# Queries and keys turned by two DMA transposes a batch, scores from 64x64 blocks in fours, a third value buffer

## The chip, the core and the metric

The kernel runs on one core of a Trainium2 chip. The metric is device time in microseconds (us); lower is better. Tensor work is done by TensorE (PE in the profile; its weight loads are listed as PEld), element-wise work by VectorE (DVE), ScalarE (ACT) and GpSimd (POOL). SyncE (SP) issues DMAs only; POOL issues DMAs as well, between its element-wise instructions. Every engine runs its own instructions strictly in the order in which the program lists them.

## The reference, cut to what matters

Sliding-window causal attention (window 64) over 8 batches, 8 heads, 576 rows, head size 64, and behind it a two-layer feed-forward block whose activation is h*cos(h), over all 8*576 = 4608 rows.

```
scores = scale * matmul(q, k.transpose(0, 1, 3, 2))
mask = (rel >= 0) & (rel < 64)            # rel = query row - key row
scores = where(mask, scores, -1e9); scores -= max(scores)
attn = exp(scores); attn = attn / (sum(attn) + 1e-9)
x = matmul(attn, v)                       # to 4608 x 512
h = x @ w_in;  g = h * cos(h);  out = g @ w_out     # 512 -> 2048 -> 512
```

Inputs and output are float32; on the chip the matmul operands are bf16.

## The kernel before, in words

**Tiles.** The feed-forward block works on nine tiles (`mt` 0 to 8) of 512 rows. A stage of the program is one `mt`: first 64 matmuls 128x128 by 512 columns that make `h_ps` (`first`, L338 to L342), each of 16 banks followed by a sine on ACT (L486) and a product on DVE (L489) that makes `gT`; then 64 matmuls of the same size that make `out_ps` (L501). I call them the h phase and the out phase. Attention of batch t+1 is woven into stage t, for t from 0 to 6: its scores, softmax and transposes run beside stage t, and its weighted values (`values`, L314) and their copies `xT` (`put_x`, L325) come at the end of the stage, as the next stage's `first` reads `xT`. Stages 7 and 8 hold no scores.

**A unit** is one batch, a pair of heads and one block of 64 query rows against 128 key rows; a batch has 9 blocks and 4 pairs, so 36 units. `groups` (L221 to L229, sizes from `CUTS`) puts 3 or 4 units together. For each group there are `g_scores` (PE, L232), `g_max` (DVE: mask and row maximum, a custom instruction for each unit, L268), `g_exp` (ACT, L279), `g_inv` (DVE), `g_norm` (POOL, L293) and `g_trans` (a DMA transpose on SP that makes `wT`, L305; for a few groups of batches 0 and 1 by PE, L302).

**How q and k get their head size onto the partitions.** Batches 0 and 1: PE transposes of 64x64 (L177). Batches 2 to 7: `load_chunk` (L142) loads q and k as 6 chunks of 96 rows each, in bf16. q is then turned by PE, 6 transposes for each pair of heads (L180), into PSUM, and two DVE copies for each pair (`put_block`, L199) write it into `qblocks`, where the two heads of a pair stand on the diagonal of a 128x128 block whose other half was set to zero (`clear`, L348, and L432). So one matmul 128x128 by 128 columns gives the scores of both heads (L248). k is turned by 6 DMA transposes on SP (`turn_k`, L212) for batches 3 to 7, by PE and ACT copies for batch 2. Batch 0 and 1 scores are made from two 64x64 matmuls a unit (L254).

**v** lies in two buffers; the rows between the loaded 128-row chunks are copied inside SBUF by `spread_v` (L156), on POOL for batches 3 to 7.

**Order.** It is written by hand. Stage 0 begins with the list `FIRST`; for the rest, `at(time, fn, ...)` (L368) puts a step into a plan, and `pump(time)` (L371), called after each sine-and-product step of the h phase and after each fourth matmul of the out phase, emits all steps that are due. A stage has `T` = 32 units of planned time, 16 for each phase, and begins at `T * mt`. So a step planned at `t0 + 14.6` stands right behind the h phase on its engine's queue. All loads are issued by POOL (in order with `g_norm`), the DMA transposes and the stores of finished rows by SP (in order with one another). PSUM has five named banks and three turning ones (`ps_t`, tag "t").

The score matmuls before, for batches 2 and up:

```
nc.tensor.matmul(out=s_ps[:, u].rearrange("p (a t) -> p a t", a=2),
                 lhsT=qblocks[(b % 2) * PAIRS + p][:, j].rearrange("d h t -> d (h t)"), rhs=rhs,
                 start=True, stop=True, skip_group_check=True)
```

Of the kernel before, what the change touches and what calls it, by code (L numbers as in the profile page):

```python
# [10 lines left out]
def _safe_warn(msg, *a, **kw):  # L11
# [12 lines left out]
NU = 9  # L24
NC, NP = 6, 96
# [3 lines left out]
CUTS = (  # L29
# [7 lines left out]
)  # L37
# [21 lines left out]
def kernel(  # L59
# [45 lines left out]
    H_BANKS = ("O1", "X0", "X1", "S", "O0") * 3 + ("X0",)  # L105
    S_BANKS = ("X1", "S", "X0")
    S_FIRST = ("O1", "S", "O0", "X0", "X1")

    def bank(which, name):
        return ps.tile([128, 512], F32, tag=which, name=name)  # L110
# [21 lines left out]
    def rows_tile(name):  # L132
        return ld.tile([128, NC * H * D], BF16, tag=name, name=name)

    def load_heads(name, b, p0=0, n=PAIRS):
        if (name, b) not in st:
            st[name, b] = rows_tile(name)[:, 0:PAIRS * RC * D].rearrange("p (a x) -> p a x", a=PAIRS)
        src = {"q": q, "k": k}[name][b, 2 * p0:2 * p0 + 2 * n]
        nc.gpsimd.dma_start(out=st[name, b][:, p0:p0 + n],
                            in_=src.rearrange("(a h) (p c) d -> (h p) a (c d)", h=2, c=RC))  # L140

    def load_chunk(name, b, c):  # L142
        if (name, b) not in st:
            st[name, b] = rows_tile(name)[0:NP].rearrange("p (c x) -> p c x", c=NC)
        src = {"q": q, "k": k}[name][b, :, c * NP:c * NP + NP]
        nc.gpsimd.dma_start(out=st[name, b][:, c].rearrange("p (h d) -> p h d", h=H),  # L146
                            in_=src.rearrange("h p d -> p h d"))

    def load_v(b, c):
        n = 128 if c < 4 else 64  # L150
        vt = vtiles[b % 2][:n, 2 * c if c < 4 else 2 * c - 1]
        nc.gpsimd.dma_start(out=vt.rearrange("p (h d) -> p h d", h=H),  # L152
                            in_=v[b, :, c * 128:c * 128 + n, :].rearrange("h p d -> p h d"))


    def spread_v(b, half, engine="p"):  # L156
        vt = vtiles[b % 2]
# [12 lines left out]
    def transposed(name, b, p):  # L170
        t_ps = ps_t.tile([128, S], BF16, tag="t", name=f"t{name}_ps")
        of = st[name, b]
        if b < 2:
            for c in range(RC):
                for h in range(2):
                    d = slice(64 * h, 64 * h + 64)
                    nc.tensor.transpose(t_ps[d, 64 * c:64 * c + 64], of[d, p, 64 * c:64 * c + 64], ident[d, d])  # L177
        else:
            for c in range(NC):
                nc.tensor.transpose(t_ps[:, NP * c:NP * c + NP], of[:, c, 128 * p:128 * p + 128], ident[:NP, :NP])  # L180
        return t_ps


    def in_order(t_ps, to, b):
        return (t_ps.rearrange("d (c p) -> d p c", c=RC), to.rearrange("d (p c) -> d p c", c=RC)) if b < 2 else (t_ps, to)

    def tr_q(b, p):
        st["tq", b, p] = transposed("q", b, p)

    def put_q(b, p, engine=None):  # L190
        of, to = in_order(st.pop(("tq", b, p)), qtiles[b * PAIRS + p], b)
        if b:
# [6 lines left out]
    def put_block(b, p, h):  # L199
        d = slice(64 * h, 64 * h + 64)  # L200
        copy("d", qblocks[(b % 2) * PAIRS + p][d, :, h], st["tq", b, p][d].rearrange("d (j t) -> d j t", j=NU))

    def tr_k(b, p):
        st["tk", b, p] = transposed("k", b, p)

    def k_tile(b):
        if ("kA", b) not in st:
            st["kA", b] = ka = att.tile([128, PAIRS, S], BF16, tag="kT", name="kT", bufs=2)
            st.update({("kT", b, p): ka[:, p] for p in range(PAIRS)})
        return st["kA", b]  # L210

    def turn_k(b, c):  # L212
        nc.sync.dma_start(out=k_tile(b)[:, :, c * NP:c * NP + NP], in_=st["k", b][:, c], transpose=True)

    def put_k(b, p, engine="a"):
        kt = k_tile(b)[:, p]
        of, to = in_order(st.pop(("tk", b, p)), kt, b)
        copy(engine, to, of)
# [13 lines left out]
    def g_scores(n, which):  # L232
        s_ps = bank(S_FIRST[which] if n < n_first else S_BANKS[which], "s_ps")
        units = groups[n]
        s_ps = s_ps[:, 0:len(units) * 128].rearrange("p (u c) -> p u c", c=128)
        if n < n_first:
            m0 = 2 if units[0][2] else 0
            nc.tensor.matmul(out=s_ps.rearrange("p u c -> p (u c)"), lhsT=ident,
                             rhs=mask16[:, m0:m0 + len(units)].rearrange("p u c -> p (u c)"),
                             start=True, stop=False, skip_group_check=True)  # L240
        for u, (b, p, j) in enumerate(units):
            kt = st["kT", b, p]
            lo = max(64 * j - 64, 0)
            rhs = kt[:, lo:lo + 128].rearrange("d (a t) -> d a t", a=2)
            if j and j % 2 == 0:
                rhs = rhs[:, ::-1, :]
            if b > 1:
                nc.tensor.matmul(out=s_ps[:, u].rearrange("p (a t) -> p a t", a=2),  # L248
                                 lhsT=qblocks[(b % 2) * PAIRS + p][:, j].rearrange("d h t -> d (h t)"), rhs=rhs,
                                 start=True, stop=True, skip_group_check=True)  # L250
                continue
            for h in range(2):
                d = slice(64 * h, 64 * h + 64)
                nc.tensor.matmul(out=s_ps[d, u].rearrange("p (a t) -> p a t", a=2),  # L254
                                 lhsT=qtiles[b * PAIRS + p][d, 64 * j:64 * j + 64], rhs=rhs[d], start=n >= n_first,
                                 stop=n >= n_first or u == len(units) - 1, skip_group_check=True)
        st["s", n] = s_ps

# [55 lines left out]
    def values(mt, p):  # L314
        st["o", mt, p] = o_ps = bank("S", "o_ps") if mt > 1 and p == PAIRS - 1 else ps_t.tile([128, MT], F32, tag="t", name="o_ps")
        for i in range(TU):
            b, j = divmod(mt * TU + i, NU)
            wT = st["wT", (b, p, j)]
            for h in range(2):
                nc.tensor.matmul(out=o_ps[64 * h:64 * h + 64, 64 * i:64 * i + 64],  # L320
                                 lhsT=vtiles[b % 2][:, max(j - 1, 0), 128 * p + 64 * h:128 * p + 64 * h + 64],
                                 rhs=wT[:, 64 * h:64 * h + 64], start=True, stop=True, skip_group_check=True)
# [15 lines left out]
    def first(mt, ff, ks, start, stop):  # L338
        if start:
            st["h", ff] = bank(H_BANKS[ff], "h_ps")  # L340
# [7 lines left out]
    def clear(i):  # L348
        nc.gpsimd.memset(qblocks[i].rearrange("d j h t -> d (j h t)"), 0.0)

    def last_rows(gT, o_sb):
        ms = MT // 128 - 1
        for which, lo, hi in (("O0", 0, LAST), ("S", LAST, d_model)):
# [26 lines left out]
    for t in range(B - 1):  # L380
        last = max(i for i, units in enumerate(groups) if units[0][0] == t + 1)
        time = T * t + Q - 1.4
        for i in range(last + 1 - n):
            time += PACE * len(groups[n - 1]) if i else 0
            at(time - 1.05 * (i % 2) * (t == 0), g_scores, n, i % 3)
# [9 lines left out]
    for b in range(1, B):  # L395
        t0 = T * (b - 1)
        for p in range(PAIRS):
            t_q = 7 + 1.8 * p if b == 1 else t0 + 1 + 2.5 * p if b == 2 else t0 + 1 + 3.5 * p
            steps = (((0, tr_q), (0.01, tr_k), (0.02, put_q), (0.03, put_k)) if b == 1 else
                     ((0, tr_q), (0.02, put_block, 0), (0.5, put_block, 1)) +  # L400
                     (((9.5 - 0.8 * p, tr_k), (9.51 - 0.8 * p, put_k)) if b == 2 else ()))
            for lag, fn, *args in steps:
                at(t_q + lag, fn, b, p, *args)
        if b > 1:
            for c in range(NC):
                for i, name in enumerate(("q", "k")):
                    at(t0 - T + (5.6 + 1.6 * c + 0.8 * i if b > 2 else 27.5 + 0.9 * c if i else 4 + 0.5 * c), load_chunk, name, b, c)
            for c in range(NC if b > 2 else 0):
                at(t0 - 5.5 + c, turn_k, b, c)
            for c in range(5):  # L410
                at(t0 + 0.5 + c, load_v, b, c)
            for half in range(2):
                at(t0 + (14.45 + 0.1 * half if b > 2 else 10), spread_v, b, half, "p" if b > 2 else "dma")
    for half in range(2):
        at(17.5, spread_v, 1, half, "dma")
    for p in range(PAIRS):
        at(T + 3 + 4 * p, clear, PAIRS + p)
# [13 lines left out]
    for t in qblocks[:PAIRS]:  # L431
# [109 lines left out]
```

## Time and profile before

| What | Value |
|---|---|
| Time, median of 3 runs (all) | 318.29 us (317.81, 318.29, 319.23) |
| Span of the profiled execution, first to last instruction | 316.6 us |
| What lies around the span, taken as median less span | 1.7 us |
| PE busy | 300.1 us, 95% of the span |
| ACT, DVE, POOL busy | 238.3, 227.8, 196.6 us |
| Start of `first` of stages 0 to 8, in us of the span | 26.43, 61.99, 95.59, 129.25, 160.59, 192.62, 224.62, 256.61, 285.63 |

The profile is of one execution of its own, for which only the span is known; the median is of other executions. The rows of a view read: line, engine, operation, tiles and shapes, count, then busy time and the mean of one instruction; "idle before" names the time that the engine stood still just ahead and what ended it. The chain of waits is the work that ended last, followed back from the last instruction; its rows are start, duration, what. Matmuls are pipelined, so the mean duration of one (379 ns for 512 columns) is longer than the distance from one to the next.

### The profile page before, as it was taken

The numbers are of one execution on the slowest core, as the hardware profiler recorded it, in microseconds if no ns is written. First come the engines' busy times: TensorE is split into PE (matmuls) and PEld (weight loads), VectorE is DVE, ScalarE is ACT, GpSimd is POOL, SyncE is SP. The second block draws the span as 40 slices with busy tenths as digits, with TensorE's granted clock in tenths as the row PEclk, the third lists the DMA queues.
The fourth block names the chain that finished last, engine by engine and source line by source line (L and its number), as shares of the span: only waits on it lengthen the run. The fifth ranks groups of instructions, "written<-read, shape, count | busy, mean of one in ns | idle before, by whom it ended". The sixth has DMA issues, their size and how long they took to land.

```text
span 316.6 us, 7858 instructions
## 1 busy us (share of the span) xinstructions
PE 300.1 (95%) x2580; PEld 157.5 (50%) x2620; DVE 227.8 (72%) x871; ACT 238.3 (75%) x789; POOL 196.6 (62%) x228
## 2 busy tenths in 40 slices
PE   3678999999999999999999999999999999999995
PEld 2544545555555544545554555555555554454443
DVE  5976778689767977697859885997599758335801
ACT  3978689868998689869986998699868996115600
POOL 8896156799969767897788878986832630000000
PEclk9979999999999999999999999999999999999999
DMA  6999996699959994899989997999692442011011
GB/s 97 170 211 207 207 148 90 70 194 162 160 92 98 151 228 85 88 153 231 124 91 140 230 123 83 158 218 127 77 179 92 81 105 100 2 66 69 0 66 66
DMA packets 150697, 39.91 MB, mean 126 GB/s; under 512 B 139392, under 2 KB 146176, under 8 KB 150656
## 3 DMA queue, kind: packets, MB, share of 16 engines
q0 software_dynamic: 99824, 18.36, 75.7%
q1 hardware_dynamic: 50688, 20.85, 32.5%
q8 instruction: 20, 0.33, 0.4%
q14 instruction: 21, 0.17, 0.2%
q10 hardware_dynamic: 144, 0.20, 0.2%
HBM read 36.70 MB, written 9.44 MB: 146 GB/s over the span
## 4 chain that ended last, share of the span: by engine, by line
PE 81%; DVE 6%; ACT 5%; POOL 3%; issue 2%; DMA 2%; POOLq 0%
PE h_ps L341 35%; PE out_ps L501 34%; ACT e L279 3%; PE s_ps L248 3%; DVE gT L489 3%; PE o_ps L320 3%; DMA k<-in_k_dram 2%; PE tq_ps L180 2%; PE s_ps L254 1%; POOL w L293 1%; PE out_ps L356 1%; DVE qB L113 1%; PE tw_ps L302 1%; POOL v L113 1%; PE tk_ps L177 1%
## 5 line engine op out<-in xcount | busy, mean ns | idle before, releaser
L341 PE MATMUL h_ps<-xT,w_in 128*128 128x512 bf16 x556 | 130.5, 379 | 2.9 <-ACT xT L113 1.0
L501 PE MATMUL out_ps<-w_out,gT 128*128 128x512 bf16 x543 | 130.9, 379 | 1.2 <-issue 0.5
L486 ACT ACTIVATE sin<-h_ps 128x512 f32<-128x512 f32 x144 | 83.6, 598 | 39.2 <-PE h_ps L341 36.2
L489 DVE TENSOR_TENSOR gT<-h_ps,sin 128x512 bf16<-128x512 f32 x144 | 92.2, 685 | 27.1 <-ACT sin L486 26.2
L279 ACT ACTIVATE e<-s,negm 128x128 f32<-128x128 f32 x256 | 98.7, 388 | 1.0 <-DVE negm L268 0.9
L293 POOL TENSOR_TENSOR w<-e,rden 128x512 bf16<-128x512 f32 (+1 forms) x78 | 74.0, 958 | 35.6 <-DVE rden L286 29.1
L341 PEld LDWEIGHTS <-w_in 128*128 128x128 bf16 x576 | 54.3, 98 | 60.7 <-issue 2.4
L501 PEld LDWEIGHTS <-gT 128*128 128x128 bf16 x560 | 51.5, 98 | 49.7
L268 DVE CUSTOM_DVE_ANT_0 s<-s_ps,mask 128x128 f32<-128x128 f32 x256 | 58.2, 285 | 1.9 <-PE s_ps L254 1.6
L279 ACT ACTIVATION_READ_ACCUMULATOR e<-s,negm 128x1 f32 x256 | 48.1, 188 | 0.0
L146 POOL DMA_DIRECT2D q<-in_q_dram x36 | 28.9, 804 | 12.3 <-PE h_ps L341 4.7
L152 POOL DMA_DIRECT2D v<-in_v_dram x40 | 34.1, 874 | 3.0 <-DMA k<-in_k_dram 2.0
L146 POOL DMA_DIRECT2D k<-in_k_dram x36 | 29.0, 806 | 3.2 <-DMA k<-in_k_dram 2.4
L113 ACT COPY out_sb<-out_ps 128x512 f32<-128x512 f32 (+1 forms) x18 | 10.1, 563 | 25.7 <-PE out_ps L501 20.2
L286 DVE RECIPROCAL rden<-den 128x4 f32<-128x4 f32 (+1 forms) x80 | 13.9, 173 | 20.9 <-ACT e L279 18.3
L113 DVE CAST xT<-o_ps 128x512 bf16<-128x512 f32 x27 | 17.5, 678 | 9.9 <-PE o_ps L320 9.9
L113 DVE COPY out_sb<-out_ps 128x512 f32<-128x512 f32 x18 | 12.4, 689 | 16.6 <-PE out_ps L501 12.6
L248 PEld LDWEIGHTS <-qB 128*128 128x128 bf16 x216 | 17.0, 98 | 14.6 <-DVE negm L268 0.6
L113 POOL COPY v<-v 64x2048 bf16<-64x2048 bf16 (+1 forms) x11 | 18.7, 1701 | 5.4 <-DMA v<-in_v_dram 5.0
L248 PE MATMUL s_ps<-kT,qB 128*128 128x128 bf16 x216 | 21.9, 219 | 0.2 <-DVE negm L268 0.2
L113 DVE COPY qB<-tq_ps 64x576 bf16<-64x576 bf16 x48 | 21.6, 450 | 0.3
L268 DVE DVE_READ_ACCUMULATOR2_ANT negm<- 128x1 f32 x256 | 21.3, 83 | 0.0
(57 smaller groups left out, 187.5 us busy)
## 6 DMA issues: line engine op xcount, KB each, us to landing
out_dram<-out_sb SPq DMA_DIRECT2D x16, 512.0 KB, 6.8
v<-in_v_dram POOLq DMA_DIRECT2D x32, 128.0 KB, 6.2
q<-in_q_dram POOLq DMA_DIRECT2D x36, 96.0 KB, 7.1
k<-in_k_dram POOLq DMA_DIRECT2D x36, 96.0 KB, 7.5
w_out<-in_moe_w_out_dram POOLq DMA_DIRECT2D x2, 1024.0 KB, 16.4
w_in<-in_moe_w_in_dram POOLq DMA_DIRECT2D x2, 768.0 KB, 11.8
wT<-w SPq DMA_TRANSPOSE x66, 2.9
out_dram<-out_sb SPq DMA_DIRECT2D x3, 256.0 KB, 2.0
```

The lines of the kernel that those rows point to most:

```text
L113: {"a": nc.scalar.copy, "p": nc.gpsimd.tensor_copy}.get(engine, nc.vector.tensor_copy)(out, in_)
L146: nc.gpsimd.dma_start(out=st[name, b][:, c].rearrange("p (h d) -> p h d", h=H), in_=src.rearrange("h p d -> p h d"))
L152: nc.gpsimd.dma_start(out=vt.rearrange("p (h d) -> p h d", h=H), in_=v[b, :, c * 128:c * 128 + n, :].rearrange("h p d -> p h d"))
L248: nc.tensor.matmul(out=s_ps[:, u].rearrange("p (a t) -> p a t", a=2), lhsT=qblocks[(b % 2) * PAIRS + p][:, j].rearrange("d h t -> d (h t)" ...
L268: nc.vector.tensor_tensor_reduce(out=s[:, u], in0=s_ps[:, u], in1=mask[:, 2 - j % 2 if j else 0], scale=-scale if b else -1.0, scalar=BIG, ...
L279: nc.scalar.activation(e[:, u], s[:, u], AF.Exp, bias=negm[:, u:u + 1], scale=1.0 if n < n_first else -1.0, accum_out=den[:, u:u + 1])
L286: nc.vector.reciprocal(out=rden[:, 0:len(groups[n])], in_=den[:, 0:len(groups[n])])
L293: (nc.gpsimd if engine == "p" else nc.vector).tensor_tensor(out=w[:, 0:u], in0=e[:, 0:u], op=ALU.mult, in1=rden[:, 0:u].unsqueeze(2).to_br ...
L341: nc.tensor.matmul(out=st["h", ff], lhsT=w_in_sb[:, ks, ff * 128:ff * 128 + 128], rhs=st["xT", mt][:, ks], start=start, stop=stop)
L486: nc.scalar.activation(sin, h_ps, AF.Sin, bias=math.pi / 2.0)
L489: nc.vector.tensor_tensor(out=gt[:, e], in0=h_ps, in1=sin, op=ALU.mult)
L501: nc.tensor.matmul(out=o_ps[e], lhsT=gT[ff // 2][:, ff % 2, ms * 128:ms * 128 + 128], rhs=w_out_sb[:, ff], start=ff == 0, stop=ff == n_ff - 1)
```

## The change

q and k of batches 2 to 7 are loaded as 128-row chunks into nine slots of one tile `rows` (slots 0 to 3 q, 5 to 8 k; slot 4 holds the last 64 rows of q on partitions 0 to 63 and those of k on 64 to 127). Two DMA transposes on SP turn the tile, slots 0 to 4 and slots 5 to 8, at planned time `t0 + 1.6` and `t0 + 1.7` of the stage that needs them. `qblocks`, `put_block`, `clear`, `turn_k` and the PE transposes of these batches go. Scores of batches 1 to 7 are made by `burst`: two groups together, each unit from two 64x64 blocks, the second group's blocks with the head halves crossed over on the output side, so that four consecutive matmuls use four different quarters of the PE array. In stages 1 to 6 there are two bursts (4 groups at `t0 + 14.6`, 6 groups 24 `out_ps` matmuls later) in place of ten single groups; in stage 0 the groups go two by two. Batch 1's PE transposes are paired in the same way. v gets a third buffer, and `spread_v` goes from POOL to DVE, at `t0 + 12.3` and `t0 + 13.3`, which puts the two copies ahead of the last two products of the h phase. The banks of `h_ps` and `out_ps` are dealt out anew.

As built, SP's order in stages 2 to 6 is: the previous batch's `wT` transposes, the two stores of 512 KB, the two turns, then this batch's ten `wT` transposes. In stage 1 the two turns stand ahead of the two stores. POOL's order in a stage is: last products of the previous batch, 5 v loads, 5 q loads, 5 k loads (for the batch that the next stage scores; none in stage 6), then the products of this batch.

```
-    qtiles = [const.tile([128, S], BF16, name=f"qT{i}") for i in range(2 * PAIRS)]
-    qblocks = [const.tile([128, NU, 2, 64], BF16, name=f"qB{i}") for i in range(2 * PAIRS)]
-    vtiles = [const.tile([128, NU - 1, d_model], BF16, name=f"v{i}") for i in range(2)]
+    vtiles = [const.tile([128, NU - 1, d_model], BF16, name=f"v{i}") for i in range(3)]
...
+CUTS = (FIRST_CUT,) + ((((1, 0, 4),), ((2, 4, 6),), ((1, 6, 9),)),) * 6
+    H_FIRST = ("O1", "X0", "X1", "S", "O0") * 3 + ("X0",)
+    H_BANKS = ("X0", "O0", "X1", "S", "O1") * 2 + ("X0", "X1", "S", "O0", "O1", "t")
+    BURSTS = (("X0", "X1", "S", "t"), ("X0", "X1", "S", "t", "t", "t"))
...
     def load_chunk(name, b, c):
+        n = 128 if c < 4 else 64
+        lo = 64 if c == 4 and name == "k" else 0
+        slot = c + (5 if c < 4 and name == "k" else 0)
+        nc.gpsimd.dma_start(out=rows(b)[lo:lo + n, slot * 512:slot * 512 + 512].rearrange("p (h d) -> p h d", h=H),
+                            in_={"q": q, "k": k}[name][b, :, c * 128:c * 128 + n].rearrange("h p d -> p h d"))
+
+    def turn(b, lo, hi):
+        nc.sync.dma_start(out=turned(b)[:, lo * 512:hi * 512].rearrange("d (g x) -> d g x", x=128),
+                          in_=rows(b)[:, lo * 512:hi * 512], transpose=True)
...
+    def burst(n0, banks):
+        for i in range(0, len(banks), 2):
+            pair = [groups[n0 + i], groups[n0 + i + 1]]
+            s_ps = [bank(which, "s_ps")[:, 0:len(pair[0]) * 128].rearrange("p (u c) -> p u c", c=128)
+                    for which in banks[i:i + 2]]
+            for u in range(len(pair[0])):
+                for cross in range(2):
+                    b, p, j = pair[cross][u]
+                    for h in range(2):
+                        d, to = slice(64 * h, 64 * h + 64), slice(64 * (h ^ cross), 64 * (h ^ cross) + 64)
+                        nc.tensor.matmul(out=s_ps[cross][to, u].rearrange("p (a t) -> p a t", a=2),
+                                         lhsT=q_cols(b, p, j)[d], rhs=k_cols(b, p, j)[d],
+                                         start=True, stop=True, skip_group_check=True)
...
+        if t:
+            at(times[0], burst, n, BURSTS[0])
+            at(times[4] + 0.1, burst, n + 4, BURSTS[1])
+        else:
+            for i in range(0, last + 1 - n, 2):
+                at(times[max(i - 1, 0)] + (0.5 if i else 0), burst, n + i, (S_BANKS[i % 3], S_BANKS[(i + 1) % 3]))
...
+    for b in range(2, B):
         t0 = T * (b - 1)
+        for c in range(NC):
+            for i, name in enumerate(("q", "k")):
+                at(t0 - T + 4 + (0 if b == 2 else 4.5) + 0.9 * (5 * i + c), load_chunk, name, b, c)
+            at(t0 + 4 + 0.9 * c, load_v, b, c)
+        at(t0 + 1.6, turn, b, 0, 5)
+        at(t0 + 1.7, turn, b, 5, 9)
+        for half in range(2):
+            at(t0 + 12.3 + half, spread_v, b, half, "d")
...
-    for t in qblocks[:PAIRS]:
-        nc.vector.memset(t.rearrange("d j h t -> d (j h t)"), 0.0)
```

More of the change, by code (lines that the diff above doesn't have):

```diff
@@ L232, in g_scores @@
     def g_scores(n, which):
-        s_ps = bank(S_FIRST[which] if n < n_first else S_BANKS[which], "s_ps")
+        s_ps = bank(S_FIRST[which], "s_ps")
         units = groups[n]
         s_ps = s_ps[:, 0:len(units) * 128].rearrange("p (u c) -> p u c", c=128)
[L236 to L240, printed above, removed]
@@ L241, in g_scores @@
-        for u, (b, p, j) in enumerate(units):
[L242 to L251, printed above, removed]
+        m0 = 2 if units[0][2] else 0
@@ L493 @@
             o_sb = moe.tile([128, 2, d_model], F32, tag="out", name="out_sb", bufs=2)
[L494 removed]
+            o_ps = [bank(which, "out_ps") for which in (("O0",) if mt == n_mt - 1 and ms0 else ("O0", "O1"))]
             for step, (lo, e) in enumerate([(lo, e) for lo in range(0, n_ff, half) for e in range(2)]):
```

164 lines of the change are left out of this document (77 added, 87 removed), and 7 rows, old and new, of the table CUTS.

## The prediction, made before the changed kernel was run

> **What bounds it now.** I read the page first, then the busy times cut at the stages, then the chain of waits inside one stage.
>
> ```profile
> PE 300.1 (95%) x2580; PEld 157.5 (50%) x2620; DVE 227.8 (72%) x871; ACT 238.3 (75%) x789; POOL 196.6 (62%) x228
> PEclk9979999999999999999999999999999999999999
> ```
>
> PE is busy 95% of the span at full granted clock, so what is taken off PE can count. The first and the last of the six stages that hold the changed work (row = start:end, length, then busy us of PE, PEld, DVE, ACT, POOL):
>
> ```profile
> 61.99:95.59 33.60, 33.35 (x305) 18.08 (x307) 26.44 (x114) 29.34 (x98) 30.68 (x36) 1.00 1.56 148
> ...
> 224.62:256.61 31.99, 31.75 (x248) 16.64 (x252) 25.75 (x113) 27.36 (x95) 17.06 (x17) 1.00 0.72 109
> ```
>
> Stages 1 to 6 take 256.61 - 61.99 = 194.6 us together, 32.4 each, and PE has work in nearly all of it (33.35 of 33.60, 31.75 of 31.99). The chain through stage 4 stays on PE all the way:
>
> ```profile
> 160.59 1.06 PE h_ps L341 x4
> ...
> 163.38 0.26 PE tq_ps L180 x6
> ...
> 175.64 0.22 PE s_ps L248 x4
> ...
> 181.71 0.17 PE s_ps L248 x3
> ...
> 188.01 3.45 PE out_ps L501 x16
> ...
> 192.62 1.02 PE h_ps L341 x4
> ```
>
> So the h phase lasts 175.64 - 160.59 = 15.05 us and the out phase 192.62 - 175.64 = 16.98. One large matmul costs 3.45 / 16 = 0.216 us. Four blocks of q transposes cost 4 * 0.26 = 1.04 us; ten score groups (six of four units, four of three) cost 6 * 0.22 + 4 * 0.17 = 2.0.
>
> ACT stands close behind PE:
>
> ```profile
> 175.68 0.60 ACT L486 ACTIVATE sin<-h_ps 128x512 f32<-128x512 f32 x1 [0.27 <-PE h_ps L341]
> 177.69 0.39 ACT L279 ACTIVATE e<-s,negm 128x128 f32<-128x128 f32 x1
> 192.03 0.57 ACT L113 COPY out_sb<-out_ps 128x512 f32<-128x512 f32 x1
> 192.49 0.58 ACT L113 CAST xT<-o_ps 128x512 bf16<-128x512 f32 x1
> ```
>
> Its exponentials start 2.05 us after the h phase's end, run without a gap to 192.03, and the `xT` copy ends at 193.07. PE needs that copy for the fourth matmul of the next stage, 3 * 0.216 = 0.65 us after 192.62: a slack of 0.2 us.
>
> **The parts, on PE and ACT.** Let S be a stage's first `h_ps` matmul and H the end of its h phase.
>
> The q transposes go in stages 1 to 6, so H = S + 14.0 in place of 15.05 (in stage 1 k's go too). Scores become 72 matmuls of 64x64 a stage. The two-at-a-time form is in stage 0:
>
> ```profile
> 34.94 0.40 PE tq_ps L177 x18
> ```
> ```profile
> 42.50 0.56 PE s_ps L254 x16
> ...
> 45.76 0.45 PE s_ps L254 x12
> ```
>
> (0.56 - 0.45) / 4 = 0.028 us a matmul, and 0.11 for entering a block. Four at a time I take half of that, as all four quarters work: 72 * 0.014 + 2 * 0.11 = 1.2 us in place of 2.0. The other end is no overlap beyond two, 72 * 0.028 + 0.22 = 2.2. The out phase on PE is then 16.2 us.
>
> In the Trainium skill, TensorEngine Tiling (Array Packing), section "Restrictions and Gotchas", speaks against this: different row tiles cannot access the same PSUM bank at the same time. By it the two row halves would go one after the other. The two-at-a-time blocks above already write one bank from both row halves, and 0.028 is half of what one 128-column matmul of the 128x128 form costs (0.22 / 4 = 0.056): the trace does not bear the rule out for this shape.
>
> ACT's work after H is unchanged. DVE gets the two v copies ahead of the last two products, and loses eight `qB` copies:
>
> ```profile
> 175.21 1.88 DVE L489 TENSOR_TENSOR gT<-h_ps,sin 128x512 bf16<-128x512 f32 x3
> ```
> ```profile
> 0.96 2.36 DVE L432 MEMSET qB<- 128x576 uint32 x4
> ```
> ```profile
> 19.09 1.23 DVE L113 COPY v<-v 64x1536 bf16<-64x1536 bf16 x1
> ```
> ```profile
> 18.75 3.33 POOL L293 TENSOR_TENSOR w<-e,rden 128x512 bf16<-128x512 f32 x3
> ```
>
> The last three products of this h phase run back to back (1.88 us), so a copy put ahead of the last two delays them by its whole length. The one DVE copy of v took 1.23 us, beside a POOL instruction that had 0.7 us left (3.33 / 3 = 1.11 each, from 18.75). If it waited for that, the copy alone is 0.5 us; if not, 1.2 and by size 1.6. I take 0.5 and 0.65, as POOL only issues DMAs at that place: the first exponential moves from H + 2.05 to about H + 2.2, and the next stage can start at H + 17.1 by ACT, H + 16.2 by PE. The high end (2.8 us) would cost 1.7 us a stage where nothing else is late. POOL's relief and the third v buffer I cost at nothing: POOL is not on the stage's chain, and its v loads start right behind the last product (below), with no wait for a v buffer. The fills that zeroed `qblocks` ran on DVE from 0.96 to 3.32, while nothing but loads was on its way; nothing too, with some tenths as the other end. Batch 1's halved blocks and transposes in stage 0 are worth 80 * 0.014 = 1.1 us and something between nothing and 4 * 0.40; I take 1.4 in all (ends 0.5 and 2.5).
>
> With every load in time a stage takes 14.0 + 17.1 = 31.1 us.
>
> **The part that decides: two big DMA transposes.** The turns are due by H, because the first burst needs both, and behind that burst the whole out phase is queued on PE. How far do they get in 14 us?
>
> ```profile
> 172.28 1.23 SPq L364 DMA_DIRECT2D out_dram<-out_sb  x2
> ```
> ```profile
> 194.28 1.20 SPq L305 DMA_TRANSPOSE wT<-w  x1
> ```
> ```profile
> 192.73 1.04 POOL L293 TENSOR_TENSOR w<-e,rden 128x512 bf16<-128x512 f32 x1 [0.95 <-DVE rden L286]
> 193.71 4.27 POOL L152 DMA_DIRECT2D v<-in_v_dram  x5
> ```
>
> The last product of a stage ends at S + 1.15, its `wT` transpose occupies SP for 1.2, the two stores for 1.23: the first turn is issued at S + 3.6. Stores and turns share SP's queue (q1). POOL issues its loads (q0) from S + 1.1 on. How the two queues share the 16 DMA engines is seen in narrow windows of the DMA view; packets and MB, first beside transposes (0.5 us), then beside the stores (2 us), then transposes alone (0.6 us), then loads alone (1 us):
>
> ```profile
> q0 software_dynamic: 218, 0.03, 84.7%
> q1 hardware_dynamic: 198, 0.05, 76.4%
> ```
> ```profile
> q1 hardware_dynamic: 310, 0.60, 89.9%
> q0 software_dynamic: 308, 0.04, 29.8%
> ```
> ```profile
> q1 hardware_dynamic: 446, 0.11, 94.7%
> ```
> ```profile
> q0 software_dynamic: 1219, 0.15, 239.7%
> ```
>
> When both have work, packets go one for one. A transpose packet is a quarter KB (0.11 MB / 446), one 128x128 block is 128 of them, the 36 blocks of both turns 4608. The loads of a stage are 13,800 packets of 128 B (three tensors of 4608), 11.3 us alone, so in stages 2 to 5 they last through the whole h phase. Then:
> stores, 512 packets of 2 KB at 155/us: S + 3.6 to S + 6.9;
> turns at (218 + 198) / 2 = 208 packets in 0.5 us, 416/us: 11.1 us, to S + 18.0.
> That is 4.0 us after H. The stage becomes 18.0 + 16.2 = 34.2 us.
> Bounds: alone, 446 / 0.6 = 743/us, the turns would take 6.2 us and land at S + 13.1, in time. By SP's issue time, if it grows with the blocks, 9 * 1.2 = 10.8 us from S + 3.6, plus landing: S + 16 at least. I take the mixed rate, since the loads are there.
> Stage 6 issues no q and k loads: the v loads end near S + 14, the rest of the turns goes at 743/us, to S + 16.4; the stage takes 32.6. Stage 1 has its turns ahead of the stores, behind only six `wT`: in time, 31.1.
>
> **Sum.** Stages 1 to 6: 31.1 + 4 * 34.2 + 32.6 = 200.5, against 194.6: +5.9. Stage 0: -1.4. Span 316.6 + 4.5 = 321; with the 1.7 us outside the span 322.8. I forecast **323 us**: PE work is saved, and the wait for the turns gives back more.
>
> **Rivals.**
> Turns in time (faster): the transposes get the engines as if alone, or the loads pause; then six stages of 31.1 = 186.6, -8.0 and -1.4: 307.2 + 1.7 = **309**. It decides from the turns landing by S + 14.9 (14.0 and the 0.9 that ACT leaves PE). For it: 743/us alone. Against: one for one in every loaded window I looked at. By the Trainium skill, DMA: Bandwidth & Descriptors, section "Latency and other measured facts", DMA transposes reach 261 GB/s; an estimate by that figure for the 1.18 MB is 4.5 us, landing at S + 11.4, which is this rival; the trace shows 0.11 MB / 0.6 us = 183 GB/s alone and about 107 GB/s mixed.
> Transposes first, v late: turns land near S + 13, but the fourth v load then near S + 15, and DVE, queued behind that v copy, starts the maxima 1.5 us late: stages 2 to 5 take 32.4: **315**.
> Slow turns: over the whole of this stage's h phase (13.9 us) q1 moved only this much, its transposes being issued singly:
>
> ```profile
> q1 hardware_dynamic: 3109, 0.74, 38.7%
> ```
>
> That is 224 packets/us. At that pace the loads have 1219 - 224 = 995/us and end 13.9 us after about S + 2.6; the turns, begun at S + 6.9, have moved 2150 packets by S + 16.5, and the other 2460 go alone at 743/us, to S + 19.8. Stages 2 to 5 then take 36.0: 4 * 1.8 more than forecast, **330**. If a big turn were held to 224/us throughout, it would be S + 27.5 and about 370.
> Fours that do not overlap: 1.0 us more in each late stage and 1.1 in stage 0: **328**.
>
> **How the numbers follow.** Turns late by about 4 us (318 to 332): 0.43. In time: 0.25. V late: 0.12. Slow turns: 0.12, a third of it beyond the range. Fours not overlapping: 0.08. Break-even of the whole is turns at S + 16.9. Half a per cent, 1.6 us, is about what a measurement of this kernel can tell from no change. Faster: 0.25 and most of v late, 0.35. Same: 0.08, from between the cases. Slower: 0.57. A PE that waits 4 us may also lose clock, as in the third and fourth slices above (0.7); that is in the upper end. Range 308 to 342; the forecast's own is 318 to 332.
>
> **What would show it.** Right: PE idle of about 4 us ahead of the first burst in stages 2 to 5, ended by a DMA into `T`, less in stage 6, none in stage 1; h phases of 14.0 us; 32 block matmuls in about 0.55 us; turns landing at S + 18 with stores moving ahead of them. Wrong: turns that land before S + 14.9; v copies on DVE that wait for a load or run over 1 us; PE waiting instead for `xT` from ACT in every stage (on time); a wait for a PSUM bank in the second burst.

## The result, and the profile after

The changed kernel takes **379.9 us** (median of 4 runs, 379.23 to 382.49) against 318.56 us for the kernel before (4 runs): a ratio of 1.194, 95% interval 1.190 to 1.198. The forecast was 323 us in a range of 308 to 342. The sign was right and the size was not: +61 us in place of +5. All medians here have all runs in them, and the ratios leave out runs more than 1.5% above the fastest of the same kernel, which are two of six and four of eight in the two kernels of "Turns and loads kept apart".

The span is 378.3 us. The page's row of busy times, and its row of the granted clock in 40 slices:

```profile
PE 299.3 (79%) x2628; PEld 147.1 (39%) x2668; DVE 218.0 (58%) x831; ACT 238.5 (63%) x785; POOL 171.4 (45%) x202
...
PEclk9999989996999599985999779985999799999999
```

PE does as much as before (299 us against 300) and stands still for 79 us. Once in each scoring stage the clock drops. The busy times by stage (start:end, length, busy us of PE, PEld, DVE, ACT, POOL, then clock): stages 0, 3 and 6, and from the kernel before its stage 0, both counted from the first `h_ps` matmul (in the table of starts, 26.43 and 129.25 are later runs of these matmuls; stages 0 and 3 of the kernel before begin at 22.18 and 128.04).

```profile
21.61:66.23 44.62, 37.40 (x441) 18.38 (x449) 30.00 (x127) 33.30 (x116) 25.61 (x30) 0.96 1.28 149
...
148.49:192.91 44.42, 31.50 (x261) 15.11 (x264) 24.64 (x107) 27.82 (x95) 22.03 (x25) 0.88 1.12 118
...
280.58:318.61 38.03, 31.91 (x261) 15.24 (x265) 24.23 (x107) 27.84 (x95) 13.66 (x15) 0.91 0.74 109
```
```profile
22.18:61.82 39.64, 37.90 (x440) 19.72 (x448) 29.65 (x127) 33.70 (x117) 22.66 (x28) 1.00 1.19 150
```

Stages 1 to 6 take 39.88, 42.38, 44.42, 43.93, 43.74 and 38.03 us, 252.4 together where 200.5 were forecast; stage 0 grew by 5.0 where it was to lose 1.4. What PE waits for, in the whole run (total, times, longest):

```profile
PE s_ps L259 <- DMA T<-rows: 57.0, 6, 12.6
PE tw_ps L309 <- POOL w L300: 6.9, 4, 5.2
```

So the step that decides is the predicted one: the first burst of every scoring stage waits for a turn. Stage 3 (S = 148.49) shows how late it comes. First SyncE's queue, then the first burst on PE with its wait in brackets:

```profile
145.61 5.84 SPq L312 DMA_TRANSPOSE wT<-w  x4
151.59 1.01 SPq L369 DMA_DIRECT2D out_dram<-out_sb  x2
153.25 15.38 SPq L154 DMA_TRANSPOSE T<-rows  x2
```
```profile
175.04 1.07 PE L259 MATMUL s_ps<-T 64*64 64x128 bf16 x32 [12.57 <-DMA T<-rows]
```

The burst starts at S + 26.55, 12.6 us behind the h phase (13.8 us long, as forecast). The DMA view of the same stage in narrow windows, packets and MB by queue: while the stores move (153 to 158.5, 5.5 us), in a standstill (160 to 161.5, 1.5 us), with turns and loads together (161.5 to 166.5, 5 us), between the first turn and the second (166.6 to 168.1, 1.5 us), and just ahead of the burst (173.5 to 175.04, 1.54 us):

```profile
q0 software_dynamic: 2112, 0.27, 75.7%
q1 hardware_dynamic: 587, 1.04, 63.0%
```
```profile
q1 hardware_dynamic: 121, 0.03, 52.7%
q0 software_dynamic: 122, 0.02, 33.7%
```
```profile
q1 hardware_dynamic: 2058, 0.53, 79.5%
q0 software_dynamic: 1933, 0.24, 74.5%
```
```profile
q0 software_dynamic: 1476, 0.19, 210.8%
q1 hardware_dynamic: 176, 0.04, 24.2%
```
```profile
q0 software_dynamic: 1860, 0.23, 238.8%
q1 hardware_dynamic: 32, 0.00, 2.9%
```

The third pair bears out the forecast's rate: 2058 / 5 = 412 packets a microsecond for the turns and 387 for the loads, nearly one for one; the forecast had 416. The Trainium skill, DMA: Bandwidth & Descriptors, section "Queues, rings and completion order", says that each DMA engine takes packets from the queues that have work in turn; the trace agrees in this pair. What the forecast lacked stands in the other pairs. The stores' 1.04 MB took until S + 10, not S + 6.9, and here it is not one for one: at 2 KB a packet they are some 510 beside 2112 of the loads. There are times in which hardly anything moves, 121 packets in 1.5 us. Between the turns the loads move nearly alone. And in the last 1.5 us ahead of the burst no packet of a turn moves any more (the 32 hold 0.00 MB), yet the burst still waits.

### The profile page after: what moved, and what is told of

The parts are those of the page before. It is cut to its first block, busy times and chain, and to the rows that moved or that the text cites. A ratio compares the mean times of both kernels' runs of the same rounds, so it can differ in the third digit from the quotient of the medians.

```text
span 378.3 us, 7842 instructions
## 1 busy us (share of the span) xinstructions
PE 299.3 (79%) x2628; PEld 147.1 (39%) x2668; DVE 218.0 (58%) x831; ACT 238.5 (63%) x785; POOL 171.4 (45%) x202
## 4 chain that ended last, share of the span: by engine, by line
PE 28%; DMA 27%; POOL 24%; issue 20%; DVE 0%; POOLq 0%
PE out_ps L505 17%; DMA rows<-in_q_dram 15%; POOL w L300 12%; PE h_ps L349 7%; POOL v L160 5%; DMA w_out<-in_moe_w_out_dram 5%; DMA T<-rows 5%; POOL rows L150 3%; DMA v<-in_v_dram 3%; POOL rows L143 2%; PE s_ps L259 1%; PE out_ps L361 1%; PE o_ps L328 1%; POOL v L108 1%; POOL w_in L173 1%
## 5 line engine op out<-in xcount | busy, mean ns | idle before, releaser
L505 PE MATMUL out_ps<-w_out,gT 128*128 128x512 bf16 x543 | 132.8, 400 | 2.5 <-issue 2.0
L349 PE MATMUL h_ps<-xT,w_in 128*128 128x512 bf16 x556 | 125.6, 379 | 2.2 <-DVE xT L108 0.6
L493 DVE TENSOR_TENSOR gT<-h_ps,sin 128x512 bf16<-128x512 f32 x144 | 95.4, 687 | 33.4 <-ACT sin L490 33.0
L505 PEld LDWEIGHTS <-gT 128*128 128x128 bf16 x560 | 55.8, 103 | 70.5 <-issue 14.6
L259 PE MATMUL s_ps<-T 64*64 64x128 bf16 x512 | 13.2, 253 | 57.0 <-DMA T<-rows 57.0
L150 POOL DMA_DIRECT2D rows<-in_k_dram x30 | 25.6, 861 | 24.4 <-DMA v<-in_v_dram 15.8
L259 PEld LDWEIGHTS <-T 64*64 64x64 bf16 x512 | 10.0, 128 | 64.6 <-issue 60.6
L150 POOL DMA_DIRECT2D rows<-in_q_dram x30 | 25.4, 886 | 15.8 <-DMA v<-in_v_dram 6.1
L108 DVE CAST xT<-o_ps 128x512 bf16<-128x512 f32 x27 | 17.5, 678 | 13.8 <-PE o_ps L328 13.8
L108 DVE COPY v<-v 64x1536 bf16<-64x1536 bf16 (+1 forms) x13 | 10.9, 836 | 5.7 <-DMA v<-in_v_dram 5.5
L286 ACT ACTIVATE e<-s_ps,negm 128x128 f32<-128x128 f32 x32 | 11.4, 408 | 1.4 <-DVE negm L271 1.4
```

What stands on the lines that cost most here:

```text
L108: {"a": nc.scalar.copy, "p": nc.gpsimd.tensor_copy}.get(engine, nc.vector.tensor_copy)(out, in_)
L150: nc.gpsimd.dma_start(out=rows(b)[lo:lo + n, slot * 512:slot * 512 + 512].rearrange("p (h d) -> p h d", h=H), in_={"q": q, "k": k}[name][b ...
L259: nc.tensor.matmul(out=s_ps[cross][to, u].rearrange("p (a t) -> p a t", a=2), lhsT=q_cols(b, p, j)[d], rhs=k_cols(b, p, j)[d], start=True, ...
L286: nc.scalar.activation(e[:, u], s[:, u], AF.Exp, bias=negm[:, u:u + 1], scale=1.0 if n < n_first else -1.0, accum_out=den[:, u:u + 1])
L349: nc.tensor.matmul(out=st["h", ff], lhsT=w_in_sb[:, ks, ff * 128:ff * 128 + 128], rhs=st["xT", mt][:, ks], start=start, stop=stop)
L493: nc.vector.tensor_tensor(out=gt[:, e], in0=h_ps, in1=sin, op=ALU.mult)
```

## The experiments

Times are medians, beside runs of the kernel before on the same chip (318.2 to 318.7 us). S is a stage's first `h_ps` matmul.

### Turns ahead of the stores

```diff
-        at(t0 + 1.6, turn, b, 0, 5)
-        at(t0 + 1.7, turn, b, 5, 9)
+        at(t0 + 0.3, turn, b, 0, 5)
+        at(t0 + 0.4, turn, b, 5, 9)
```

> The two turns are planned ahead of the two stores in stages 2 to 6 (t0 + 0.3 and 0.4 in place of t0 + 1.6 and 1.7); nothing else. Theory, the turns are late because they queue behind the stores and then share the DMA engines with the loads: their first packet moves at about S + 3.5 in place of S + 10, the rest lasts as before (15 us), so the first burst begins near S + 20 in place of S + 26, stages 2 to 5 take about 38 and stage 6 about 34, the whole about 352 us (345 to 360). Rival, a big turn takes its 15 us on SP whatever stands beside it: only the 1.2 us that SP needs for the two stores are won, landing at S + 24, about 374 us.

Measured: **355.8 us**, ratio 1.118 (1.114 to 1.121). The stage that starts at 145.75, and stage 6:

```profile
145.75:186.63 40.88, 33.37 (x264) 15.45 (x264) 24.16 (x107) 27.83 (x95) 22.29 (x25) 0.87 1.25 128
...
263.39:294.58 31.19, 30.45 (x264) 14.54 (x264) 24.17 (x107) 26.75 (x94) 13.76 (x15) 1.00 0.86 130
```

The first bursts start at S + 20.0 to 21.5 in stages 2 to 5. The stores ahead cost 24 us of the 61. Stage 6, which has no q and k loads beside its turns, is at the full-speed length of 31.2; its turns land at S + 14.6.

### The turns without loads

```diff
-                at(t0 - T + 4 + (0 if b == 2 else 4.5) + 0.9 * (5 * i + c), load_chunk, name, b, c)
-            at(t0 + 4 + 0.9 * c, load_v, b, c)
+                if b == 2:
+                    at(t0 - T + 4 + 0.9 * (5 * i + c), load_chunk, name, b, c)
+            if b == 2:
+                at(t0 + 4 + 0.9 * c, load_v, b, c)
...
-                          in_=rows(b)[:, lo * 512:hi * 512], transpose=True)
+                          in_=rows(2)[:, lo * 512:hi * 512], transpose=True)
```

> Leaves out the loads of q, k and v of batches 3 to 7; the turns of these batches turn the rows of batch 2 again, with the same packets. The stores stay ahead of the turns. Theory, sharing with the loads: the stores are gone by S + 7, the 4608 packets of the turns go at about 1000 a microsecond with 1 to 2 us of pauses, the first burst begins near S + 14, stages 1 to 6 take 31 to 32.5 us each, the whole about 319 us (314 to 326, with stage 0 unchanged). Rival, the turns are slow by themselves (15 us on SP from S + 4.4, 2.5 us to landing): the first burst begins near S + 22, stages of 39, about 360 us.

Measured: **317.1 us**, ratio 0.996 (0.994 to 0.998); most loads are left out here, so this is not a faster kernel. PE's waits for the turns, the DMA view between 139.5 and 144 (4.5 us, turns alone), its SyncE queue, and the stage that starts at 129.97:

```profile
PE s_ps L259 <- DMA T<-rows: 2.7, 3, 1.2
```
```profile
q1 hardware_dynamic: 3626, 0.91, 109.4%
```
```profile
135.24 7.09 SPq L154 DMA_TRANSPOSE T<-rows  x2
```
```profile
129.97:161.28 31.31, 30.83 (x264) 14.63 (x264) 24.21 (x107) 27.37 (x95) 9.55 (x10) 1.00 0.50 111
```

Alone the turns run at 3626 / 4.5 = 806 packets a microsecond, without a pause in this stage (about 1000 were expected), and PE's wait for them falls from 57.0 to 2.7 us. The turns are not slow by themselves: with the stores ahead and nothing else they are just in time, and stages 2 to 6 take 31.2 to 31.6 us, where the forecast gave 31.1 for that case. SyncE's hold falls with them, 15.4 us for both turns in the changed kernel, 7.1 here.

### Two directions one behind the other, and no crossing

```diff
-            for u in range(len(pair[0])):
-                for cross in range(2):
+            for cross in range(2):
+                for u in range(len(pair[0])):
```

> The same 64x64 score matmuls, but those of the second group of a pair behind those of the first, so that two consecutive matmuls use two quarters of the array and not four. Theory, four at a time take half of two at a time: a burst of 40 takes about 1.25 us in place of 0.75, that of 32 at half clock about 1.9 in place of 1.07; 1.3 us a stage in stages 1 to 6 and about 1 us in stage 0, about 388 us (385 to 391). Rival, the crossed order brings nothing beyond two at a time: bursts as long as now, 380 us within 1.

Measured: **380.0 us**, ratio 1.193 (1.190 to 1.196), no change. The second kernel leaves the order and takes the crossing out:

```diff
-                        d, to = slice(64 * h, 64 * h + 64), slice(64 * (h ^ cross), 64 * (h ^ cross) + 64)
+                        d, to = slice(64 * h, 64 * h + 64), slice(64 * h, 64 * h + 64)
...
-                    st["cross", (b, p, j)] = cross ^ (p % 2 if b == 1 else 0)
+                    st["cross", (b, p, j)] = p % 2 if b == 1 else 0
```

> The second group of a pair is not crossed over: all 64x64 score matmuls use only the two quarters on the diagonal, as in the kernel before; the order stays. Theory, the halved time per matmul (14 ns against 28 in stage 0 of the kernel before) comes from the use of all four quarters somewhere in the burst: the 40 matmuls of the second burst take 1.1 us from first to last in place of 0.54. Rival, it comes from something else (the layout in one tile, the order): 0.54 as with the crossing. The whole is within 2 us of 380 by the rival and about 384 by the theory.

Measured: **384.8 us** (382.9 to 386.6), ratio 1.209 (1.202 to 1.216). The second burst on PE in the changed kernel, with the two directions one behind the other, and without crossing:

```profile
182.26 0.75 PE L259 MATMUL s_ps<-T 64*64 64x128 bf16 x40
```
```profile
138.94 0.77 PE L259 MATMUL s_ps<-T 64*64 64x128 bf16 x40
```
```profile
138.16 1.30 PE L259 MATMUL s_ps<-T 64*64 64x128 bf16 x40
```

The crossing is worth (1.30 - 0.75) / 40 = 14 ns a matmul, half of the 28: the forecast's 0.014 us is right, and so is its reason, four quarters. The first kernel does not test the reason, as I had thought it would: there six or eight matmuls of one direction stand ahead of as many of the other, and they cost no more than when they alternate. How PE overlaps matmuls that stand so far apart was not found.

### Turns a stage earlier

Both turns of batches 3 to 7 go behind the loads, ahead of `wT` of the stage before; the k loads of batch 2 go behind the products of stage 0.

```diff
-                at(t0 - T + 4 + (0 if b == 2 else 4.5) + 0.9 * (5 * i + c), load_chunk, name, b, c)
+                at(t0 - T + ((4, 27.5)[i] + 0.9 * c if b == 2 else 8.5 + 0.9 * (5 * i + c)), load_chunk, name, b, c)
...
+        at(t0 + 0.3 if b == 2 else t0 - T + 16.8, turn, b, 0, 5)
+        at(t0 + 0.4 if b == 2 else t0 - T + 16.9, turn, b, 5, 9)
```

> The two turns of batches 3 to 7 go to the out phase of the stage before (behind the last load of q and k on the plan, ahead of that stage's transposes of w), those of batch 2 ahead of the stores of stage 1; the loads of k of batch 2 go behind the products w of stage 0, as in the kernel before. Theory: the loads then run without turns beside them and end near S + 15, the turns run alone and land by about S + 23, PE does not wait for T in stages 2 to 6; these take 31.5 to 33.5 us, stage 1 still about 38, stage 0 loses its 5 us: about 323 us (315 to 335). Rival, the turns hold SP for 15 us whatever stands beside them: the transposes of w of the same stage come 10 us late and the stages take about 38: 350 us.

Measured: **336.6 us**, ratio 1.058 (1.055 to 1.061). PE's waits, and SyncE's queue in stage 2:

```profile
PE s_ps L259 <- DMA T<-rows: 10.1, 1, 10.1
PE o_ps L328 <- DMA wT<-w: 9.7, 12, 2.6
```
```profile
124.79 5.20 SPq L154 DMA_TRANSPOSE T<-rows  x2
130.08 12.28 SPq L312 DMA_TRANSPOSE wT<-w  x8
```

Only stage 1 waits for a turn now. In stages 2 to 5 (33.5 to 35.1 us) the turns stand in front of `wT`, whose first one starts at S + 24.7 to S + 26.6, where it starts at S + 19.6 to S + 19.8 in the run without loads, and the values wait for the last. Stage 0 is 38.83 us: the 5 us that it had lost came from the k loads ahead of the products `w` on POOL.

In a second form the first turn goes there and the second ahead of the stores; the last k chunk is loaded first (and the other four of batch 2 between the products of stage 0):

```diff
-                at(t0 - T + 4 + (0 if b == 2 else 4.5) + 0.9 * (5 * i + c), load_chunk, name, b, c)
+                at(t0 - T + (22 + 1.5 * c if b == 2 and i and c < 4 else (4 if b == 2 else 8.5) + 0.9 * (c if not i else 5 if c == 4 else 6 + c)), load_chunk, name, b, c)
...
-        at(t0 + 1.6, turn, b, 0, 5)
-        at(t0 + 1.7, turn, b, 5, 9)
+        at(t0 - T + (17.6 if b == 2 else 16), turn, b, 0, 5)
+        at(t0 + 0.3, turn, b, 5, 9)
```

> The first turn of a batch (slots 0 to 4) goes to the out phase of the stage before, ahead of that stage's transposes of w; the second (slots 5 to 8) goes to the start of the stage that needs it, ahead of the stores. The last chunk of k is loaded ahead of the other four, as the first turn needs it; the four other k loads of batch 2 go between the products w of stage 0. Theory, sharing and queue order: the first turn runs when the loads are nearly done and lands near S + 21, when the first transpose of w is due; the second, 2048 packets at 415 a microsecond from S + 3, lands near S + 10. PE does not wait for T in stages 1 to 6, the transposes of w come on time: stages 2 to 6 of 31.2 to 32, stage 1 of 32 to 34, stage 0 of 39.5, together 314 us (310 to 319). Rival, the first turn still delays the transposes of w by 3 us as in the kernel that moves both: 327 us.

Measured: **326.3 us**, ratio 1.025 (1.023 to 1.027); stages 5 and 6 are 31.3 us, but in stages 2 to 4 the second turn starts behind late `wT` at S + 5 to S + 7, shares with the loads and lands at S + 16 to S + 19. It lies at the rival's 327, though through the late second turn more than through `wT`:

```profile
PE s_ps L259 <- DMA T<-rows: 9.4, 3, 5.4
...
PE o_ps L328 <- DMA wT<-w: 0.9, 1, 0.9
```

### PE kept busy while it waits

```diff
+            if len(banks) == 4 and i == 0:
+                mt = pair[0][0][0] - 1
+                for _ in range(48 if 2 <= mt <= 5 else 20):
+                    nc.tensor.matmul(out=s_ps[0].rearrange("p u c -> p (u c)"), lhsT=w_in_sb[:, 0, 0:128],
+                                     rhs=st["xT", mt][:, 0, 0:128 * len(pair[0])], start=True, stop=True,
+                                     skip_group_check=True)
```

> Adds work that nothing reads: 48 matmuls of 128x128 by 512 or 384 columns (20 in stages 1 and 6) ahead of the first burst, into a bank that the burst then overwrites, so that PE computes for most of the time in which it waits for the turns. Theory, the standing PE loses its clock and pays for it after the wait: with a busy PE the first burst takes 0.65 us in place of 1.0 and the 23 matmuls behind it 5.0 in place of 6.3; 1.6 us a stage in stages 1 to 6, 370 us (368 to 373). Rival, the low clock has another cause than the standing: 380 us, or more where the added work ends later than the turns.

Measured: **368.0 us** (364.95 to 368.83), ratio 1.158 (1.156 to 1.160): 12 us less by more matmuls. Stage 3 from its first burst on: in the changed kernel the first 4 us and the rest, then the same in this kernel (column behind POOL: granted clock):

```profile
175.04:179.00 3.96, 3.91 (x41) 2.02 (x43) 2.85 (x25) 2.90 (x15) 0.89 (x1) 0.63 1.08 72
179.00:192.91 13.91, 13.72 (x160) 6.89 (x159) 8.27 (x61) 12.83 (x61) 7.74 (x9) 1.00 0.35 70
```
```profile
166.90:171.00 4.10, 4.09 (x49) 2.11 (x49) 2.85 (x25) 3.25 (x17) 1.03 (x1) 1.00 1.08 71
171.00:183.42 12.42, 12.39 (x154) 6.24 (x153) 8.42 (x61) 12.28 (x59) 7.59 (x8) 1.00 0.39 78
```

17.87 us from burst to next stage there, 16.52 here: 1.35 us in this stage, and 1.8 as a mean of stages 2 to 5 (18.3 against 16.5). That is the price of standing still beyond the wait itself, 11.7 us of the 61 over stages 1 to 6. The changed kernel's clock in stage 3, in windows of 2 us:

```profile
166.00:168.00 2.00, 0.00 (x0) 0.00 (x0) 1.10 (x2) 0.00 (x0) 0.50 (x1) 0.93 2.20 151
...
176.00:178.00 2.00, 2.00 (x9) 0.74 (x6) 1.64 (x17) 1.90 (x10) 0.00 (x0) 0.51 0.98 68
178.00:180.00 2.00, 1.95 (x9) 0.88 (x9) 0.93 (x9) 2.00 (x13) 1.03 (x1) 1.00 0.00 0
```

PE stands still from 162.5 to 175.0. The clock fell about 5 us into the wait (166 to 168 us have a mean of 0.93, the next windows 0.50) and was back 3 us behind the burst, and 6 us behind it in a stage of the kernel with the turns first. The Trainium skill, TensorE: Matmul & The Clock Gate, section "What's actually happening", has the clock at half after about 3.4 us without work and back after about 3.4 us of work; here it was about 5 us to the fall and 3 to 6 us to the recovery.

### Nine small turns

```diff
-        at(t0 + 1.6, turn, b, 0, 5)
-        at(t0 + 1.7, turn, b, 5, 9)
+        for i9 in range(9):
+            at(t0 + 1.6 + 0.01 * i9, turn, b, i9, i9 + 1)
```

> The two turns are cut into nine of four 128x128 blocks each, at the same place. Theory, packets share the DMA engines one for one whatever the size of the transpose: the last lands at S + 24 to S + 27 as now, 380 us (375 to 386). Rival, the pauses inside and between the big turns come from their size: without them the last lands 3 us earlier in stages 2 to 5, 365 us; or nine issues cost more than two, 390 us.

Measured: **380.8 us** (380.0 to 381.5), ratio 1.196 (1.193 to 1.199): cutting the turns small does not bring them in earlier, so their size is not the cause.

### Turns and loads kept apart

q and k of batches 2 to 7 have one buffer, so that the next loads wait for both turns; the turns go to t0 - 0.8; v is loaded a stage earlier, between the products `w`.

```diff
-            st["rows", b] = ld.tile([128, 2 * PAIRS * S], BF16, tag="rows", name="rows")
+            st["rows", b] = ld.tile([128, 2 * PAIRS * S], BF16, tag="rows" if b < 2 else "rows2", name="rows",
+                                    bufs=2 if b < 2 else 1)
...
+            at(t0 + 4 + 0.9 * c if b == 2 else t0 - T + 19 + 2.2 * c, load_v, b, c)
+        at(t0 - 0.8, turn, b, 0, 5)
+        at(t0 - 0.79, turn, b, 5, 9)
```

> Keeps turns and loads apart. The rows of batches 2 to 7 get one buffer in place of two, so that the loads of q and k of the next batch wait until both turns have read it; the turns go ahead of the last transpose of w of the stage before and ahead of the stores; v of batches 3 to 7 is loaded one stage earlier, between the products w of the out phase; the k loads of batch 2 go behind the products of stage 0 but for the last chunk. Theory, turns alone: 4608 packets at about 1000 a microsecond and 1 to 2 us of pauses, from about S + 1 to S + 8; the loads run after them and are issued by S + 18, when the first product w is due; PE waits for T in no stage, and stages 1 to 6 take 31.2 to 32 as without loads: 312 us (308 to 317), which is faster than the kernel before. Rival, the loads, now behind the turns on POOL, delay the products w by 2 to 5 us a stage: 325 us.

Measured: **329.5 us** (326.3 to 332.1), ratio 1.031 (1.027 to 1.035). Stages 3 to 6 are 31.8, 32.3, 31.8 and 31.2 us; stages 1 and 2 are 42.0 and 37.0, since the turns of batch 2 wait for its k loads, land at S + 16.9 and so hold the next loads, and the products behind them, on POOL. The start was mended, against this kernel:

```diff
-                at(t0 - T + (27.5 + 0.9 * c if b == 2 and i and c < 4 else
+                at(t0 - T + (22 + 1.5 * c if b == 2 and i and c < 4 else
...
-            at(t0 + 4 + 0.9 * c if b == 2 else t0 - T + 19 + 2.2 * c, load_v, b, c)
+            at(t0 - T + (28 + 0.9 * c if b == 2 else 19 + 2.2 * c), load_v, b, c)
```

> The kernel that keeps turns and loads apart, with a mended start: the four late k loads of batch 2 are issued between the products w of stage 0 instead of behind them, and v of batch 2 behind these products instead of at the start of stage 1. Theory: the turns of batch 2 then find their rows landed and land by S + 9 of stage 1 in place of 16.9, POOL is free for the next loads 7 us earlier, and the products of stage 1 and the transposes of w behind them are on time: stage 1 of 33 in place of 42, stage 2 of 32 in place of 37, stage 0 of 40 in place of 38.3; 317 us (314 to 321). Rival, the loads between the products of stage 0 delay these as much as they save later: 325 us.

Measured: **324.4 us** (319.6 to 327.3), ratio 1.009 (1.006 to 1.012). Its waits, and stage 3:

```profile
PE o_ps L329 <- DMA wT<-w: 6.6, 5, 3.5
PE tw_ps L310 <- POOL w L301: 5.2, 4, 2.0
PE s_ps L260 <- DVE negm L276: 4.8, 6, 1.1
```
```profile
132.38:163.56 31.18, 30.63 (x269) 14.56 (x265) 24.11 (x105) 25.65 (x93) 20.99 (x24) 1.00 1.52 160
```

No wait for a turn is left, the clock is 1.00 in stages 1 to 6, and stage 3 takes the 31.2 us of a stage without waits. Stages 1 and 2 still take 36.3 and 33.4. What is left is waits for `wT`, for the products on POOL and for DVE's maxima; the loads stand ahead of the products and between them on POOL, and so `wT` comes late in some stages. No version tried here that does all the work is faster than the kernel before.

## Why the prediction was wrong in size

Against the forecast, stages 2 to 5 took 38 us more, stage 1 took 9, stage 0 took 6 and stage 6 took 5.

**Stage 0** (forecast -1.4, measured +5.0): the forecast costed PE there and not POOL. In the changed kernel ten loads of batch 2 stand ahead of the first product, in the kernel before six; then PE's first transpose of `w` waits:

```profile
43.14 3.32 POOL L150 DMA_DIRECT2D rows<-in_q_dram  x4 [5.09 <-DMA w_out<-in_moe_w_out_dram]
46.41 4.22 POOL L150 DMA_DIRECT2D rows<-in_k_dram  x5
50.58 2.12 POOL L300 TENSOR_TENSOR w<-e,rden 128x512 bf16<-128x512 f32 x2
```
```profile
46.63 1.05 POOL L293 TENSOR_TENSOR w<-e,rden 128x512 bf16<-128x512 f32 x1
```

The product starts 4 us later than in the kernel before (second fence). The part-by-part working followed what the moved loads do to the DMA engines, and not what queues behind them on POOL. With the k loads behind the products ("Turns a stage earlier") the stage took 38.83 us, 0.8 less than before: so much of the 1.4 was there.

**h phase, scores**: right. H is S + 13.8 (14.0 forecast); bursts cost 14 ns a matmul, and one of 32 took 0.64 us at full clock (0.55 forecast). The stage with its turns in time takes 31.2 us, where 31.1 was forecast.

**v copies**: not right, though it cost nothing here. The prediction had named as a sign of being wrong that they wait for a load or run over 1 us, and in stage 3 they did both (0.5 and 0.65 us forecast):

```profile
164.00 0.68 DVE L108 COPY v<-v 64x1536 bf16<-64x1536 bf16 x1 [1.91 <-DMA v<-in_v_dram]
165.31 1.10 DVE L108 COPY v<-v 64x2048 bf16<-64x2048 bf16 x1
```

The first copy waited 0.3 to 1.9 us for its load in stages 2 to 6. The first burst came 3 to 9 us behind the second copy, so nothing hung on it; in the kernel with the turns first the copies did not wait.

**Turns in stages 2 to 5**: due at S + 18.0 by the forecast, first burst at S + 24.4, 26.6, 25.6 and 24.8, 7.4 later as a mean. The step that failed is "stores, 512 packets of 2 KB at 155/us: S + 3.6 to S + 6.9; turns at (218 + 198) / 2 = 208 packets in 0.5 us, 416/us: 11.1 us, to S + 18.0". The rate of the turns holds while both queues move. By the packets of the trace, as means of the four stages, three terms were wrong. The stores move from S + 5.1 and the first packet of a turn at S + 10.1: 3.2 us late, 1.5 from the later start and 1.7 because the stores took 5.0 us in place of 3.3. The 155/us had been read where stores and loads moved one for one; here the loads moved about four packets for each of the stores. From there to the last packet it is 13.8 us and not 11.1: the turns start slowly or stand still for a while, and between the first and the second they stop for 1 to 2 us. And from the last packet to the burst it is another 1.4 us, which the sum had at nothing. A rate from a half-microsecond window was carried over 11 us as if it were never interrupted. What the interruptions are is open. The standstill was not found in the run without loads. A gap between the turns is there without loads too, but smaller: in stage 4 of that run 454 packets moved in one microsecond (172.4 to 173.4), in place of 806.

**Behind the burst** the stage took 18.3 us as a mean and not 16.2: 1.8 of it the clock, the rest an out phase that takes 16.5 at full clock. The forecast named the clock and put it in the range's upper end, without a price; it had read 0.7 off the third and fourth slices, where only the third shows 7. Together that is 9.4 us a stage (43.6 measured as a mean, 34.2 forecast).

**Stage 1** (31.1 forecast, 39.88 measured): "in time" was wrong, since the turns, though ahead of the stores, share with the loads of batch 3 as in all other stages; they were issued at S + 3.7 and landed at S + 20.4. By the forecast's own rate, which it did not apply there, S + 3.7 and 11.1 us make S + 14.8, the very edge of what is in time. The rest is the same terms: the first packet moves near S + 6, the last at S + 19.2, and the burst starts at S + 20.6. **Stage 6** (32.6 forecast, 38.03 measured): the same stores, landing and clock, with only the v loads beside.

**The rivals**: "slow turns" had 370 us in a side clause, from 224 packets a microsecond. The mean here, 4608 from S + 4.8 to S + 26.4 in stage 3, is 213, but its reason, a turn that is slow whatever moves beside it, is refuted by the run without loads: that it came near the time is luck. Turns in time did not occur in any stage. Transposes first, v late: v was late, with its copy at S + 15.5 in stage 3, but the turns were not first; the queues shared, and both were late. Fours that do not overlap: refuted by the 14 ns.

## What to carry to other kernels

A transfer that a whole stage waits for wants to be costed with everything that is in flight beside it, and its queue's earlier entries and the pauses priced from windows as long as the transfer itself. Where an engine issues loads in order with its own work, moving loads moves that work: look for what is next in its queue before looking at the DMA engines. And a long wait on PE costs more than itself: here the clock halved some 5 us into it, and the work behind each took 1.8 us more.

## What the runs showed that I had not expected

- SyncE's hold for the same 36 blocks depends on what else moves: 7.1 us without loads, 10.9 with the turns ahead of the stores, 15.4 behind stores and beside loads. In the kernel before one `wT` of four blocks held it 1.2 us.
- With both queues at work the DMA engines move 412 + 387 = 799 packets a microsecond; the loads alone moved 1219 (kernel before) and the turns alone 806 (run without loads). So the turns lose half their rate and the loads two thirds, and sharing is dearer than going one behind the other: as an estimate from these rates, what moves in 1 us shared would take 412 / 806 + 387 / 1219 = 0.83 us. The rate alone is not fixed: in stage 6 of the changed kernel, once the loads were done, the turns moved 1130 packets in 1 us (297.5 to 298.5).
- Small transposes and big ones share alike: nine turns of four blocks took as long in all, 380.8 us against 379.9, as two big ones.
